# A head's 64 channels on 64 partitions from batch 3 on: VectorE and GpSimd exchange odd and even channels, one load for each head of a pair

## The chip, the cores and the metric

The kernel runs on one core of a Trainium2 chip. The metric is the time of one execution in microseconds on the device. The profile is of one execution, with times counted from the start of its span, which runs from the first to the last instruction. TensorE does the matrix products; its weight loads are listed beside its matmuls as an engine of their own (PEld). ScalarE (ACT) does exponentials, the activation and most copies out of PSUM, VectorE (DVE) transposes, masks and normalises, GpSimd (POOL) adds and converts, and SyncE (SP) issues transfers, as GpSimd does for its own queue.

## The reference

Inputs are `q`, `k` and `v` of shape 8 batches x 8 heads x 576 positions x 64 channels, and two weights, 512 x 2048 and 2048 x 512. For each batch and head two attentions are added, and the sum, with the heads side by side, goes through a two-layer network:

```
q_d, k_d, v_d = means over each 4 positions               # 144 positions
out_up    = repeat(softmax(scale * q_d k_d^T) v_d, 4)     # every position with every one
out_local = softmax(scale * q k^T, only |i - j| < 4) v    # a narrow band
x = (out_up + out_local), heads beside each other         # 4608 tokens x 512
out = gelu_quick(x @ w_in) @ w_out                        # h * sigmoid(1.702 h)
```

## The kernel before, in words

**Groups.** The network works on nine groups of 512 tokens. A group g is 16 steps of `mm1` (four matmuls each, `w_in` against `xT`, then an activation into `gT`), then 64 matmuls of `mm2` (`gT` against `w_out`, four rows of output, 16 matmuls each). All engines run in the order in which the program lists their instructions (a manual schedule); nothing is reordered by a planner. The attention of batch b = g + 1 is laid into group g: a dictionary `steps` holds functions by step number, 0 to 15 for the steps of `mm1` and 16 to 80 for the matmuls of `mm2`, and each function is listed ahead of its step. `POS` (L893) gives the steps of the six parts of an attention, `POS_G` exceptions by group: scores of the first four heads (`qd` 0) at 13, their exponentials and masks at 16, scores and exponentials of the other four heads at 35, then the two value products with their normalisation at 44 and 58, then a change of the activation table at 65. Work for the next batch that is listed outside `steps` stands ahead of the group's matmuls on its engine.

**Scores.** `load_1` (L187) brings four heads of q or k, 4 x 576 x 64 numbers, into a tile of 128 partitions x 1152: a head on 32 partitions, each with 18 positions of 64 channels, converted to bf16 on the way. `prep_1` (L265) has VectorE transpose 32 x 32 blocks of pairs of channels (as 32-bit words). Then tile `kT` or `qT` holds on partition 32 r + d, for each position, the channels 2d and 2d + 1 of head r. A score therefore needs two matmuls with 32 rows, even channels then odd channels, added in PSUM (`score`, L365). `scores_mixed` (L409) lists for four heads 5 chunks x 2 halves (`par`) of the band, 64 keys x 60 queries, and 3 chunks of the means, 64 keys x 144 queries (`score_d`, L382), each twice: 80 + 24 = 104 matmuls. They sit in eight tiles of the array, four of 32 rows by two of 64 columns.

**What feeds them.** `pool_qk` (L293) has GpSimd add four positions to one, for k into `kdT` and for q into `qdT`. `prep_v` (L307) converts v to bf16, `prep_v4` (L311) adds v by fours, both on GpSimd. In the body for a later batch b (L1018 to L1031) the order is: `prep_v(b)`, the transposes and sums of `qd` 0, the loads of batch b + 1 (`load_v` on SP's queue, four of `load_1` on GpSimd's), the transposes and sums of `qd` 1, `prep_v4(b)`. The loads `load_v4(b + 1)` (SP's queue, 12 transfers) are listed one step after the last part of the attention, at 66.

The buffers that matter: `kb`/`qb` (loaded) two each by `qd`; `kT`, `qT`, `qdT` one each by `qd`; `vf` and `v4` one each; converted `vbs` and `vds` two each, by the batch's parity. PSUM has three pairs of banks (`PA`) for the attention and two banks (`PM`) for the network.

Of the kernel before, what the change touches and what calls it, by code (L numbers as in the profile page):

```python
# [9 lines left out]
BF16 = mybir.dt.bfloat16  # L10
# [9 lines left out]
def kernel(  # L20
# [16 lines left out]
    n_ffc = d_ff // 128  # L37
    n_groups = B * S // TG
    inv_sqrt_d = 1.0 / math.sqrt(D)
    KSTART = (0, 56)  # L40
    QSTART = (0, 60)

# [144 lines left out]
    def load_1(name, src, store, b, qd):  # L187
        t = ldp.tile(
            [128, 1152], BF16, name=f"{name}b{qd}", tag=f"{name}b{qd}", bufs=2
        )  # L190
        nc.gpsimd.dma_start(
            out=t,
            in_=bass.AP(
                tensor=src.tensor, offset=src[b, 4 * qd].offset,
                ap=[[1152, 128], [1, 1152]],
            ),
        )
        store[b, qd] = t

    def load_qk(b, qd):  # L200
        load_1("k", k, kf, b, qd)
# [63 lines left out]
    def prep_1(name, b, qd):  # L265
# [6 lines left out]
        )  # L272
        dst[b, qd] = tt

    def prep_qk(b, qd):
        prep_1("k", b, qd)
        prep_1("q", b, qd)
# [30 lines left out]
        cp = eng.copy if eng is nc.scalar else eng.tensor_copy  # L308
        cp(out=vbs[b % 2][:, i, h, 0:D], in_=vf[b][:, i, h])  # L309

    def prep_v4(b, eng):  # L311
        for kc in range(3):
            x = v4[0:112, kc].rearrange("p h (f d) -> p h f d", f=4)
            t1 = work.tile([128, HP, 2, D], FP32, name="v2", tag="v2")
            eng.tensor_tensor(  # L315
                out=t1[0:112], in0=x[:, :, 0:2, :], in1=x[:, :, 2:4, :], op=ALU.add
            )
            eng.tensor_tensor(
                out=vds[b % 2][0:112, kc, :, 0:D],
                in0=t1[0:112, :, 0, :], in1=t1[0:112, :, 1, :], op=ALU.add,  # L320
            )
# [87 lines left out]
    def scores_mixed(b, qd, sp, sd):  # L409
        for i in range(5):  # L410
            for a in range(2):
                if i >= 2:
                    for r in range(4):
                        score_d(b, qd, sd, i - 2, a, r)
                for x in (1, 0):
                    for r in range(4):
                        score(b, qd, sp, i, a, (side(b, r)[0] + x) % 2, r)

    def exp_local(qd, sp):
        for u in range(2):  # L420
# [227 lines left out]
    def attention(b, slots=None):  # L648
        st = {}

        def s_pe(qd):
            if slots:
                st["s", qd], st["d", qd] = [ps_tile(), ps_tile()], ps_tile()
            else:
                st["s", qd], st["d", qd] = PA[1:3], PA[0]
            scores_mixed(b, qd, st["s", qd], st["d", qd])

        def s_act(qd):
            if qd == 0:
# [12 lines left out]

        def avn(*hps):
            def f():
                for hp in hps:
                    st["o", hp] = av(b, hp, slots and slots[hp % 2])
                for hp in hps:
                    st["y", hp] = normalise(st["o", hp])
            return f

        def tr():
            for u in range(2):
                st["x", u], st["x", u + 2] = x_pair(slots and slots[u])
# [206 lines left out]
        for f in steps.get(n, ()):  # L890
            f()

    POS = [13, 16, 35, 44, 58, 65]  # L893
    POS_G = {0: [16, 18, 29, 46, 58, 67], 5: [13, 16, 35, 48, 61, 66]}
    VDP_0 = 41

    o, y, x = {}, {}, {}
# [98 lines left out]
    for g in range(n_groups):  # L996
        b = g + 1
        if g == 0:
# [75 lines left out]
```

## Time and profile before

| What | Value |
|---|---|
| Three runs | 311.63, 314.28, 315.88 us; median 314.28 |
| Profiled execution | 311.98 us, of which span 310.2 us |
| Busy share of the span | PE 96%, ACT 67%, PEld 49%, POOL 44%, DVE 38% |
| One group with attention (122.20 to 154.44 us) | 32.24 us |
| TensorE clock granted | 0.999 of full |
| 32-row matmuls of scores (all batches) | 1280 of 32x60 and 384 of 32x144 |
| Queue of GpSimd's transfers | 18336 packets, 14.81 MB |

Rows of groups read: line, engine, operation, written tile `<-` read tiles, shape, count, busy time in us, mean ns of one, and then the idle time of the engine just ahead of them with what ended it. In a timeline the columns are start, length, engine, line, operation and count. A matmul's end is modelled and matmuls overlap, so starts are read, not ends.

### The profile page before, as it was taken

The numbers are of one execution on the slowest core, as the hardware profiler recorded it, in microseconds if no ns is written. First come the engines' busy times: TensorE is split into PE (matmuls) and PEld (weight loads), VectorE is DVE, ScalarE is ACT, GpSimd is POOL, SyncE is SP. The second block draws the span as 40 slices with busy tenths as digits, with TensorE's granted clock in tenths as the row PEclk, the third lists the DMA queues.
The fourth block names the chain that finished last, engine by engine and source line by source line (L and its number), as shares of the span: only waits on it lengthen the run. The fifth ranks groups of instructions, "written<-read, shape, count | busy, mean of one in ns | idle before, by whom it ended". The sixth has DMA issues, their size and how long they took to land.

```text
span 310.2 us, 9588 instructions
## 1 busy us (share of the span) xinstructions
PE 297.4 (96%) x4140; PEld 152.8 (49%) x4183; DVE 119.4 (38%) x273; ACT 209.1 (67%) x349; POOL 137.7 (44%) x168
## 2 busy tenths in 40 slices
PE   7789999999999999999999999999999999999995
PEld 3465445455544555445545554545454544444444
DVE  5983626801592149303850286026901630000000
ACT  5557771867886788768966896688858876316611
POOL 8764790479149920992089216932492000000000
PEclk9999999999999999999999999999999999999999
DMA  6999999899959933995299609991620110010011
GB/s 135 147 200 208 178 134 212 161 193 244 175 176 194 189 90 114 193 187 124 83 199 201 136 36 203 207 168 39 165 58 35 39 70 0 34 68 36 0 68 68
DMA packets 64650, 40.07 MB, mean 129 GB/s; under 512 B 44640, under 2 KB 56032, under 8 KB 64608
## 3 DMA queue, kind: packets, MB, share of 16 engines
q0 software_dynamic: 18336, 14.81, 34.4%
q1 hardware_dynamic: 45600, 24.46, 33.5%
q8 instruction: 32, 0.52, 0.8%
q10 hardware_dynamic: 672, 0.20, 0.3%
q14 instruction: 10, 0.08, 0.1%
HBM read 44.83 MB, written 9.44 MB: 175 GB/s over the span
## 4 chain that ended last, share of the span: by engine, by line
PE 91%; DVE 2%; DMA 2%; issue 2%; ACT 1%; POOL 0%; ACTq 0%; POOLq 0%
PE pm L864 36%; PE pm L800 36%; PE pa L800 4%; PE pa L745 4%; PE pa L369 3%; PE pa L385 2%; DMA qb<-in_q_dram 2%; PE pa L864 2%; PE pm L879 1%; DVE qT L269 1%; ACT od L614 1%; PE pm L644 0%; DVE kT L269 0%; DVE qdT L288 0%; DVE kdT L288 0%
## 5 line engine op out<-in xcount | busy, mean ns | idle before, releaser
L800 PE MATMUL pm<-xT,w_in_bf 128*128 128x512 bf16 x496 | 118.2, 379 | 1.6 <-ACT xT L607 0.5
L864 PE MATMUL pm<-w_out_bf,gT 128*128 128x512 bf16 x505 | 114.6, 379 | 3.3 <-issue 3.2
L811 ACT ACTIVATE gT<-pm 128x512 bf16<-128x512 f32 x128 | 76.3, 598 | 43.5 <-PE pm L800 43.5
L800 PEld LDWEIGHTS <-w_in_bf 128*128 128x128 bf16 x576 | 55.6, 98 | 67.0 <-issue 1.2
L864 PEld LDWEIGHTS <-gT 128*128 128x128 bf16 x560 | 52.8, 98 | 61.8 <-issue 0.5
L435 DVE TENSOR_TENSOR es<-es,mask 128x600 bf16<-128x600 bf16 x28 | 14.2, 510 | 95.6 <-ACT es L421 94.5
L849 ACT ACTIVATE osb<-pm 128x512 f32<-128x512 f32 (+2 forms) x35 | 20.2, 581 | 24.4 <-PE pm L864 19.0
L299 POOL TENSOR_TENSOR pq<-kT 128x576 f32<-128x576 bf16 x13 | 15.1, 1164 | 45.8 <-DVE kT L269 45.8
L763 DVE TENSOR_TENSOR xT<-pa,r 128x300 bf16<-128x300 f32 (+3 forms) x96 | 24.0, 303 | 19.5 <-ACT r L758 19.2
L309 POOL CAST vb<-vf 128x2560 bf16<-128x2560 f32 x6 | 13.9, 2320 | 31.8 <-DMA vf<-in_v_dram 19.9
L421 ACT ACTIVATE es<-pa 128x600 bf16<-128x600 f32 x32 | 19.7, 668 | 9.0 <-PE pa L369 8.9
L757 ACT ACTIVATE r<-pa 128x504 f32<-128x504 f32 (+1 forms) x36 | 20.6, 572 | 4.3 <-PE pa L745 4.3
L315 POOL TENSOR_TENSOR v<-v 112x512 f32<-112x512 f32 x18 | 23.0, 1280 | 0.0
L758 ACT ACTIVATE r<-r 128x504 f32<-128x504 f32 (+1 forms) x36 | 22.2, 616 | 1.1
L269 DVE STREAM_TRANSPOSE kT<-kb 128x576 f32<-128x576 f32 x16 | 19.9, 1245 | 6.3 <-DMA kb<-in_k_dram 6.2
L851 DVE TENSOR_SCALAR osb<-pm 128x128 f32<-128x128 f32 x1 | 0.3, 292 | 55.4 <-ACT osb L849 55.4
L269 DVE STREAM_TRANSPOSE qT<-qb 128x576 f32<-128x576 f32 x16 | 19.8, 1239 | 0.5 <-DMA qb<-in_q_dram 0.5
L800 PE MATMUL pa<-xT,w_in_bf 128*128 128x512 bf16 x63 | 19.6, 379 | 0.0
L369 PEld LDWEIGHTS <-kT 32*64 32x64 bf16 x1280 | 14.6, 104 | 8.0 <-issue 4.5
L369 PE MATMUL pa<-qT,kT 32*64 32x60 bf16 x1280 | 16.8, 198 | 1.7 <-DVE qT L269 1.5
L771 DVE TENSOR_TENSOR xT<-xT,ydt 128x576 bf16<-128x576 bf16 x24 | 17.9, 787 | 0.0
L222 POOL DMA_DIRECT2D vb<-in_v_dram x18 | 12.3, 697 | 8.8 <-DMA w_in_bf<-in_moe_w_in_dram 3.6
(105 smaller groups left out, 288.7 us busy)
## 6 DMA issues: line engine op xcount, KB each, us to landing
out_dram<-osb SPq DMA_DIRECT2D x35, 256.0 KB, 3.0
vf<-in_v_dram SPq DMA_DIRECT2D x61, 128.0 KB, 6.4
v<-in_v_dram SPq DMA_DIRECT2D x72, 96.0 KB, 3.2
kb<-in_k_dram POOLq DMA_DIRECT2D x16, 288.0 KB, 7.4
qb<-in_q_dram POOLq DMA_DIRECT2D x16, 288.0 KB, 9.0
w_in_bf<-in_moe_w_in_dram POOLq DMA_DIRECT2D x4, 512.0 KB, 7.7
w_out_bf<-in_moe_w_out_dram POOLq DMA_DIRECT2D x4, 512.0 KB, 12.3
vb<-in_v_dram POOLq DMA_DIRECT2D x18, 64.0 KB, 6.6
```

The source lines that it names most:

```text
L269: nc.vector.transpose(out=t32.rearrange("p (i c) -> p c i", c=18), in_=store[b, qd].bitcast(FP32).rearrange("p (c d) -> p c d", c=18),)
L315: eng.tensor_tensor(out=t1[0:112], in0=x[:, :, 0:2, :], in1=x[:, :, 2:4, :], op=ALU.add)
L369: nc.tensor.matmul(sp[r // 2][64 * par : 64 * par + 64, r % 2, 60 * i : 60 * i + 60], lhsT=kT[b, qd][rows, k0 : k0 + 64, a], rhs=qT[b, qd] ...
L421: nc.scalar.activation(out=es[2 * qd + u][:, :, 0:300], in_=sp[u][:, :, 0:300], func=AF.Exp, scale=inv_sqrt_d,)
L757: nc.scalar.activation(out=r, in_=den, func=AF.Ln)
L758: nc.scalar.activation(out=r, in_=r, func=AF.Exp, scale=-1.0)
L763: nc.vector.tensor_tensor(out=sub(x[u], t0 + at, (114, n), (1, c)), in0=sub(src, c0, (60, n), (1, c)), in1=sub(rc, c0, (60, n), (1, c)), o ...
L771: nc.vector.tensor_tensor(out=xx, in0=xx, in1=yd[:, u, :, None].to_broadcast([128, SD, 4]), op=ALU.add,)
L800: nc.tensor.matmul(acc, lhsT=w_in_bf[:, dmc, ffc * 128 : (ffc + 1) * 128], rhs=xT[dmc][:, g * TG : g * TG + TG], start=(dmc == 0), stop=(d ...
L811: nc.scalar.activation(out=gT[:, ffc, :], in_=acc, func=AF.Silu, scale=GELU_SCALE)
L849: eng.activation(out=osb, in_=ap, func=AF.Copy, scale=1.0 / GELU_SCALE)
L864: nc.tensor.matmul(ops[t], lhsT=gT[:, ffc, t * 128 : (t + 1) * 128], rhs=w_out_bf[:, ffc, :], start=(ffc == 0), stop=(ffc == n_ffc - 1),)
```

## The change

From batch 3 on (`WIDE = 3`) the four heads of a quarter tile stand otherwise. Each `kb` or `qb` tile is now loaded by two transfers, each of 64 partitions: transfer j brings heads j and j + 2 of the four. After the transpose the first 32 of these partitions hold head j, the next 32 head j + 2, with even and odd channels as before. `keep_odd` has GpSimd copy the odd channels of all 128 partitions aside. `swap` has VectorE copy the even channels of head j + 2 over the odd channels of head j, and then the kept odd channels of head j over the even channels of head j + 2, with partitions shifted by 32. Then place u = 0, 1 of a position holds all 64 channels of head 2u + j on 64 partitions. `scores_64` needs one matmul of 64 rows for each product: 40 for the band and 12 for the means, 52 instead of 104, in four tiles of 64 x 64.

The work is listed in another order: the transposes, `keep_odd` and `prep_v` of the next batch's first half stand at step 17 of the group before (after the masks of `qd` 0), and the loads for them first in that group; `swap` and the sums come at the start of the group; the loads of `qd` 1 stand at the end of GpSimd's work; `prep_v4` is split around the sums of `qd` 1; `load_v4` moves from step 66 to 48; scores of `qd` 1 move from step 35 to 34, and group 5 loses its own positions (48, 61, 66 become 44, 58, 65). For the odd copies and the shifted copies of ten halves (batches 3 to 7) 20 instructions come to GpSimd and 80 to VectorE, and GpSimd issues 20 transfers more.

```diff
+    WIDE = 3
@@ load_1
+        if b < WIDE:
+            nc.gpsimd.dma_start(out=t, in_=bass.AP(... ap=[[1152, 128], [1, 1152]]))
+            return
+        for j in range(2):
+            nc.gpsimd.dma_start(
+                out=t[64 * j : 64 * j + 64],
+                in_=bass.AP(
+                    tensor=src.tensor, offset=src[b, 4 * qd + j].offset,
+                    ap=[[2 * S * D, 2], [1152, 32], [1, 1152]],
+                ),
+            )
@@
+    def keep_odd(b, qd):
+        for name, src in (("k", kT), ("q", qT)):
+            t = work.tile([128, S], BF16, name="odd", tag="odd")
+            nc.gpsimd.tensor_copy(out=t, in_=src[b, qd][:, :, 1])
+            odd[name] = t
+
+    def swap(b, qd):
+        for name, src in (("k", kT), ("q", qT)):
+            tt = src[b, qd]
+            for p in (0, 64):
+                nc.vector.tensor_copy(out=tt[p : p + 32, :, 1], in_=tt[p + 32 : p + 64, :, 0])
+            for p in (0, 64):
+                nc.vector.tensor_copy(out=tt[p + 32 : p + 64, :, 0], in_=odd[name][p : p + 32])
@@
+    def scores_64(b, qd, sp, sd):
+        def local(u, j, par, i):
+            rows = slice(64 * j, 64 * j + 64)
+            k0, q0 = 114 * i + KSTART[par], 114 * i + QSTART[par]
+            nc.tensor.matmul(
+                sp[u][64 * par : 64 * par + 64, j, 60 * i : 60 * i + 60],
+                lhsT=kT[b, qd][rows, k0 : k0 + 64, u],
+                rhs=qT[b, qd][rows, q0 : q0 + 60, u],
+                start=True, stop=True, tile_position=(64 * j, 64 * par),
+            )
+
+        def down(u, j, kc):
+            rows = slice(64 * j, 64 * j + 64)
+            nc.tensor.matmul(
+                sd[64 * u : 64 * u + 64, j, SD * kc : SD * kc + SD],
+                lhsT=kdT[qd][rows, 48 * kc : 48 * kc + 64, u],
+                rhs=qdT[b, qd][rows, :, u],
+                start=True, stop=True, tile_position=(64 * j, 64 * u),
+            )
+
+        for u in range(2):
+            for i in range(5):
+                for x in range(2):
+                    for j in range(2):
+                        local(u, j, (j + x) % 2, i)
+        for kc in range(3):
+            for x in range(2):
+                for j in range(2):
+                    down((j + x) % 2, j, kc)
@@ attention
-            scores_mixed(b, qd, st["s", qd], st["d", qd])
+            (scores_mixed if b < WIDE else scores_64)(b, qd, st["s", qd], st["d", qd])
@@
-    POS = [13, 16, 35, 44, 58, 65]
-    POS_G = {0: [16, 18, 29, 46, 58, 67], 5: [13, 16, 35, 48, 61, 66]}
+    POS = [13, 16, 34, 44, 58, 65]
+    POS_G = {0: [16, 18, 29, 46, 58, 67], 1: [13, 16, 35, 44, 58, 65]}
@@ body of a group
-        elif b < B:
-            if g > 1:
-                prep_v(b, nc.gpsimd)
+        elif b < WIDE:
             prep_qk(b, 0)
             pool_qk(b, 0)
-            if g == 1:
-                prep_v(b, nc.gpsimd)
-            if b + 1 < B:
-                load_v(b + 1)
-                for qd in range(NQ):
-                    load_qk(b + 1, qd)
+            load_qk(b + 1, 0)
+            prep_v(b, nc.gpsimd)
+            load_v(b + 1)
             prep_qk(b, 1)
             pool_qk(b, 1)
             prep_v4(b, nc.gpsimd)
+            load_qk(b + 1, 1)
+        elif b < B:
+            if b + 1 < B:
+                load_qk(b + 1, 0)
+                load_v(b + 1)
+            swap(b, 0)
+            pool_qk(b, 0)
+            prep_qk(b, 1)
+            keep_odd(b, 1)
+            swap(b, 1)
+            prep_v4(b, nc.gpsimd, (0,))
+            pool_qk(b, 1)
+            prep_v4(b, nc.gpsimd, (1, 2))
+            if b + 1 < B:
+                load_qk(b + 1, 1)
@@ steps
-                steps.setdefault(pos[-1] + 1, []).append(lambda: load_v4(b + 1))
+                for n, f in (
+                    (17, lambda: prep_qk(b + 1, 0)),
+                    (17, lambda: keep_odd(b + 1, 0)),
+                    (17, lambda: prep_v(b + 1, nc.gpsimd)),
+                    (48, lambda: load_v4(b + 1)),
+                ):
+                    steps.setdefault(n, []).append(f)
```

More of the change, by code (lines that the diff above doesn't have):

```diff
@@ L190, in load_1 @@
         )
[L191 to L197, printed above, removed]
-        store[b, qd] = t
+        store[b, qd] = t
+        if b < WIDE:
+            nc.gpsimd.dma_start(
+                out=t,
+                in_=bass.AP(
+                    tensor=src.tensor, offset=src[b, 4 * qd].offset,
+                    ap=[[1152, 128], [1, 1152]],
+                ),
+            )
+            return
+        for j in range(2):
+            nc.gpsimd.dma_start(
+                out=t[64 * j : 64 * j + 64],
+                in_=bass.AP(
+                    tensor=src.tensor, offset=src[b, 4 * qd + j].offset,
+                    ap=[[2 * S * D, 2], [1152, 32], [1, 1152]],
+                ),
+            )
     def load_qk(b, qd):
@@ L273, in prep_1 @@
         dst[b, qd] = tt
+    odd = {}
+    def keep_odd(b, qd):
[10 more added lines that the diff above has]
+                nc.vector.tensor_copy(out=tt[p + 32 : p + 64, :, 0], in_=odd[name][p : p + 32])
     def prep_qk(b, qd):
@@ L309, in prep_v, with prep_v4 @@
         cp(out=vbs[b % 2][:, i, h, 0:D], in_=vf[b][:, i, h])
-    def prep_v4(b, eng):
-        for kc in range(3):
+    def prep_v4(b, eng, kcs=range(3)):
+        for kc in kcs:
             x = v4[0:112, kc].rearrange("p h (f d) -> p h f d", f=4)
@@ L417, in scores_mixed @@
                         score(b, qd, sp, i, a, (side(b, r)[0] + x) % 2, r)
+    def scores_64(b, qd, sp, sd):
[15 more added lines that the diff above has]
+                start=True, stop=True, tile_position=(64 * j, 64 * u),
+            )
+        for u in range(2):
[7 more added lines that the diff above has]
+                    down((j + x) % 2, j, kc)
     def exp_local(qd, sp):
```

## The prediction

> **What bounds the kernel.** First the page's busy shares and the chain that ended last.
>
> ```profile
> span 310.2 us, 9588 instructions
> PE 297.4 (96%) x4140; PEld 152.8 (49%) x4183; DVE 119.4 (38%) x273; ACT 209.1 (67%) x349; POOL 137.7 (44%) x168
> ...
> PE 91%; DVE 2%; DMA 2%; issue 2%; ACT 1%; POOL 0%; ACTq 0%; POOLq 0%
> ```
>
> TensorE is on the chain for 91% of the span; VectorE and GpSimd are nowhere on it between 60 and 306 us. So time is won where TensorE's own work shrinks, and lost where one of the others makes it wait. Two slices of the busy time by stretch, both from group 3 (122.20 to 154.44 us, batch 4), show a score stage:
>
> ```profile
> 133.35:134.33 0.98, 0.98 (x105) 0.94 (x104) 0.00 (x0) 0.60 (x1) 0.98 (x1) 1.00 1.11 205
> 141.13:142.15 1.02, 1.02 (x105) 0.98 (x105) 0.00 (x0) 0.42 (x1) 0.00 (x0) 1.00 0.63 138
> ```
>
> Columns are stretch, length, then busy time and count of PE, PEld, DVE, ACT, POOL, clock, DMA share, GB/s. Each stretch goes from the first weight load of the scores to the first weight load of the dense matmuls behind. I took the same stretch, by the weight loads of the timeline, for the ten score stages of batches 3 to 7: 0.98, 1.11, 0.98, 1.02, 1.04, 0.98, 0.99, 0.99, 0.98, 0.99, together 10.06 us. That is all that the change can shrink.
>
> **The score stage, before.** In the timeline twelve matmuls with their weight loads (8 of the band, 4 of the means) repeat every 0.100 to 0.105 us, as in
>
> ```profile
> 101.40 0.23 PE L385 MATMUL pa<-qdT,kdT 32*64 32x144 bf16 x2
> ...
> 101.50 0.24 PE L385 MATMUL pa<-qdT,kdT 32*64 32x144 bf16 x2
> ...
> 101.60 0.24 PE L385 MATMUL pa<-qdT,kdT 32*64 32x144 bf16 x2
> ```
>
> that is 8.4 ns for a matmul, however many columns it has; the 32 band matmuls ahead of them start at 101.04 and the next part at 101.31, 8.4 ns each too. So the pace is one of instructions, 4.2 ns each, and 104 x 8.4 = 0.87 us; the other 0.11 us of 0.98 is the end of the stage.
>
> **The score stage, after.** 52 matmuls in four tiles of 64 x 64. The trace has that form in the value product of batch 1:
>
> ```profile
> 46.63 0.34 PE L443 MATMUL pa<-vb,es 64*64 64x65 bf16 x17
> ...
> 46.99 0.33 PE L443 MATMUL pa<-vb,es 64*64 64x65 bf16 x17
> ```
>
> These are the first matmuls of two lots of forty: 0.36 us, 9 ns each, 36 ns for each tile's turn. The columns alone take less: a dense matmul of 512 columns comes every 0.216 us (29 in 6.26 us on the chain), 2.37 columns a ns, so 65 take 27 ns. The 40 band matmuls (60 columns) cost 40 x 9 = 0.36 us. The 12 of the means put three of 144 columns on each tile; 3 x 144 / 2.37 = 0.18 us, and in the later value products (L745) twelve such start between 144.73 and 144.95, 0.22. I take 0.20. With the same 0.11 at the end: 0.67 us. Ten stages: 10.06 - 6.7 = **3.4 us less**. Ends: columns alone, (600 + 432) / 2.37 = 0.435 + 0.11 = 0.55, gives 4.6 us; the whole L745 stage's pace, 76 matmuls in 1.09 us (144.20 to 145.29), 14.3 ns each, gives 0.75 and 2.6 us. The value taken is the one from the row with the same columns.
>
> One rule of the Trainium skill speaks against this step (TensorE: Matmul & The Clock Gate, Part 3): weight loads overlap running matmuls only in another row group, and the change halves the row groups. By it the stage would lengthen only where neighbours share rows; the listed order alternates the two row halves, as that of L443 does, whose 9 ns show the overlap, so the trace bears the sum out here.
>
> **What is added beside TensorE.** Rows:
>
> ```profile
> L435 DVE TENSOR_TENSOR es<-es,mask 128x600 bf16<-128x600 bf16 x28 | 14.2, 510 | 95.6 <-ACT es L421 94.5
> L480 DVE TENSOR_TENSOR y<-pa,rc 128x896 bf16<-128x896 f32 x4 | 4.4, 1090 | 0.1
> L763 DVE TENSOR_TENSOR xT<-pa,r 128x3 bf16<-128x3 f32 x24 | 3.7, 152 | 0.0
> L309 POOL CAST vb<-vf 128x2560 bf16<-128x2560 f32 x6 | 13.9, 2320 | 31.8 <-DMA vf<-in_v_dram 19.9 <-DMA out_dram<-osb 10.4 <-DMA v<-in_v_dram 1.6
> L299 POOL TENSOR_TENSOR pq<-qT 128x576 f32<-128x576 bf16 x14 | 16.0, 1145 | 0.1
> ```
>
> VectorE's shifted copy of 32 x 576 is not in the trace. L480 and L763 give (1090 - 152) / 893 = 1.05 ns for an element and 149 ns: 0.75 us; L435 at 510 ns for 600 is the fast end, some 0.50. Back-to-back operations start 0.13 to 0.16 us sooner than their lengths say (transposes of 1.24 us start 1.08 apart). I take 0.65 from start to start, near the slow end, since the elements are not dense. GpSimd's odd copy: 0.6 by L309 (0.9 ns an element), 1.15 by L299; I take 0.8.
>
> The group of batch 4, in us after its start, where transposes now stand from 122.31 to 126.81 and then VectorE is idle for 12.95 us:
> - VectorE: normalisation of the batch before ends at +0.2 (the last L771). Swap of `qd` 0, eight copies, to +5.4; transposes of `qd` 1 to +7.6.
> - GpSimd: sums (1.15 + 0.67) of k +2.8 to +4.7, of q +5.4 to +7.2. Score stage 0 needs them at +11.2: 4 us to spare. Odd copies of `qd` 1 to +8.8.
> - VectorE: swap of `qd` 1 from +8.0 to +13.2. Masks come behind it only at +17.5 (139.75), so nothing queues.
> - GpSimd: first third of `prep_v4` (1.27 + 0.73) to +10.8, sums of k to +12.7, of q +13.2 to **+15.1**. Score stage 1 stood at +18.9 (141.13); one step of 0.22 and 0.33 of the first stage earlier, +18.4: **3.3 us to spare**.
> - GpSimd then: two thirds of `prep_v4` to +19.1, four issues of 0.57 to +21.4 (two tiles in two transfers each), odd copies of the next batch to +23 (their transposes, behind the masks, end at +20.8), `prep_v` 2.3 to +25.3, four issues to +27.6. The group lasts 31.6.
>
> So 16 x 0.65 on VectorE (13.8 busy in 32.24 now) and 4 x 0.8 plus 4 x 0.57 on GpSimd (17.5 now) cost nothing while they lie in idle time. The transposes at step 17 stand ahead of the second masks (143.19) and of the normalisation (146.07); they would have to be over 2 us late to move these. The issue waits of SP: `vf` is now free a third of a group earlier (its conversion ends at +25.3), `load_v4` waits for `prep_v4` at +19.1 and is listed at about +22, so the stores behind it do not wait. Positions 34 for 35, and group 5's, only move matmuls past each other: nothing, with 0.3 us either way.
>
> **Sum.** 311.98 (profiled execution) - 3.4 = 308.6. The profiled execution lies 2.3 below the median of the runs (314.28), whose spread is 4.25; on the median's footing the time is **310.9**.
>
> **Rivals.**
> 1. *The stage doesn't shrink.* If the four tiles run one behind another more than L443 shows, 52 matmuls cost up to 19 ns each and nothing is won: 313.5 to 314.3. For it: half as many tiles; against it: L443.
> 2. *It shrinks more.* Behind the second score stage the first dense matmul starts 0.23 us after its weight load (142.15, 142.38), which may be TensorE's queue of 208 instructions; with the columns-only stage, 0.55, that makes 4.6 + 5 x 0.23 = 5.8 less: 308.5.
> 3. *The second swap is late* (the case that ends slower). VectorE and GpSimd disturb each other:
>
> ```profile
> 75.16 1.54 DVE L435 TENSOR_TENSOR es<-es,mask 128x600 bf16<-128x600 bf16 x2 [13.37 <-ACT es L421]
> 75.54 0.84 POOL L318 TENSOR_TENSOR vd<-v 112x256 bf16<-112x256 f32 x1
> ...
> 76.33 1.49 POOL L315 TENSOR_TENSOR v<-v 112x512 f32<-112x512 f32 x1
> ```
>
> Two masks take 1.03 us undisturbed, 1.54 here; GpSimd's take 0.72 and 1.27 undisturbed. With copies 1.5 times (0.97) and GpSimd 1.2 times as long wherever both work: q of `qd` 0 swapped at +6.7, odd copies to +10.8, `qd` 1 swapped from +9.9 to +17.7, its sums at +19.9, 1.5 us late in each of five groups: 7.5 - 3.4 = +4.1, **318.4**. It decides from a copy of some 0.85 us on. Against it: that everything is disturbed at once.
> 4. *A load is late.* Two transfers of 144 KB where one of 288 KB was. Now a load lands in 4.7 to 12.8 us (median 7.4 for kb), four of them taking 21.1% of 16 engines for 33 us, 14 engine-us for a half. If a half ran on two engines only, that is 7 us alone, 14 beside as much other traffic; `qd` 1 has from +21.4 to the next group's +5.4, 15.6 us, and 3.3 to spare behind. Beyond 19 us it costs: 22 us would give 5 x 3 - 3.4, 325.9. The Trainium skill (DMA: Bandwidth & Descriptors, Rules for kernel authors, and How many engines) advises one transfer over 128 partitions against two halves, and takes the number of engines to divide both patterns' slowest dimension, here 2 of the source; no run here shows that yet.
>
> **Chances.** Forecast 0.72; (1) 0.09; (2) 0.05; (3) 0.09; (4) 0.05. What a measurement here can tell from no change is about 2%, 6.3 us: 308.0 and 320.6. The forecast's own ends, 309.7 to 311.7, widen by the runs' spread, about 2 either way, and by a footing between the profiled execution and the median. The range reaches from 306.8 (rival 2 on the faster footing) to 316.0 (half of rival 3): it leaves out most of (3) and (4). Faster by over 2%: 0.08 (half of (2), and the forecast on a faster footing). Slower: 0.08 (the worse half of (3) and most of (4)). Within: 0.84.
>
> **What will show it.** Score stages of batches 3 to 7 as one line group of 64 x 64, 400 of 60 columns and 120 of 144, weight load to dense weight load 0.67 us; groups of 31.6 instead of 32.2 to 32.5. Sums of q for `qd` 1 over 2 us ahead of the second stage. No wait of TensorE for kT, qT or qdT. A copy line over 0.85 us, a kb landing over 16 us, or such a wait on the chain would make the prediction wrong.

## The result

The changed kernel takes 316.71 us (median of 18 runs, 315.18 to 317.9) against 313.62 us (18 runs, 311.63 to 315.88): 1.0096 times as long, interval 1.0071 to 1.0121. Forecast were 310.9 us and a gain; the time lies above the range. Both profiled executions are some 1.6 us below their medians (before 311.98, after 315.19), so the two traces may be set against each other. The page of the changed kernel, its counts and the chain that ended last:

```profile
span 313.4 us, 8712 instructions
...
PE 301.9 (96%) x3663; PEld 149.3 (48%) x3663; DVE 197.7 (63%) x353; ACT 208.6 (67%) x349; POOL 173.0 (55%) x208
...
PE 64%; DVE 16%; POOL 8%; issue 4%; DMA 3%; ACT 3%; POOLq 0%; DVEq 0%; ACTq 0%
```

TensorE held 91% of the chain before and holds 64% now; VectorE and GpSimd, which had 2%, have 24%. VectorE's busy time rose from 119.4 to 197.7 us. Its 80 copies take 60 of these 78; the rest is old work that became longer.

Where the 3 us went, by the first dense matmul of each group (us):

| | group 2 starts | group 2 | 3 | 4 | 5 | 6 | behind |
|---|---|---|---|---|---|---|---|
| before | 89.91 | 32.34 | 32.24 | 32.51 | 32.39 | 32.18 | 58.6 |
| after | 90.05 | **36.13** | 31.99 | 32.10 | 32.10 | 32.41 | 58.6 |
| forecast | | 31.6 | 31.6 | 31.6 | 31.6 | 31.6 | |

Against the forecast's 31.6 group 2 loses 4.5 us and the four others 0.4, 0.5, 0.5 and 0.8: 6.7 us, which is the gap from -3.4 to +3.2. So two losses are to be explained.

**The score stage itself** did as forecast. Two stretches from the first weight load of the scores to the next dense one (columns as in the prediction), and the matmuls of the first:

```profile
137.34:137.99 0.65, 0.65 (x54) 0.54 (x53) 0.62 (x2) 0.55 (x1) 0.65 (x1) 1.00 1.05 247
144.57:145.28 0.71, 0.71 (x54) 0.60 (x53) 0.71 (x1) 0.71 (x3) 0.71 (x1) 1.00 0.00 0
```

```profile
137.34 0.52 PE L450 MATMUL pa<-qT,kT 64*64 64x60 bf16 x40
137.68 0.37 PE L459 MATMUL pa<-qdT,kdT 64*64 64x144 bf16 x12
137.99 0.39 PE L857 MATMUL pm<-xT,w_in_bf 128*128 128x512 bf16 x1
```

0.34 us for the forty of the band, 0.31 to the next dense one, 0.65 where 0.98 had been.

**Group 2.** GpSimd's timeline there (start, length, engine, line, operation; in brackets its idle time ahead and what ended it):

```profile
93.16 2.32 POOL L336 CAST vb<-vf 128x2560 bf16<-128x2560 f32 x1 [11.18 <-DMA out_dram<-osb]
95.43 1.31 POOL L203 DMA_DIRECT2D kb<-in_k_dram  x2
96.71 1.53 POOL L203 DMA_DIRECT2D qb<-in_q_dram  x2
98.23 1.18 POOL L326 TENSOR_TENSOR pq<-kT 128x576 f32<-128x576 bf16 x1
...
101.95 0.66 POOL L291 COPY odd<-kT 128x576 bf16<-128x576 bf16 x1
...
109.68 1.43 POOL L326 TENSOR_TENSOR pq<-qT 128x576 f32<-128x576 bf16 x1 [0.94 <-DVE qT L300]
111.19 0.77 POOL L330 TENSOR_TENSOR qdT<-pq 128x288 bf16<-128x288 f32 x1
```

Listed in group 1, the conversion of v of batch 3 starts only 3.1 us into group 2, after 11.18 us of waiting (the brackets name an output transfer; the chain has a transfer from 88.36 to 93.18 just ahead, and the last load of v was issued at 88.3). Behind it stand four issues, the first sums at 98.23, forecast at 92.9, the odd copies of `qd` 1, the exchange that needs them (VectorE 102.64 to 109.60) and the last sum, done at 111.96. The means of the second score stage start at 112.01. The pause also cost clock, the share of TensorE's full speed that it was granted. The same columns as above, in stretches of 1 us:

```profile
111.00:112.00 1.00, 0.00 (x0) 0.00 (x0) 1.00 (x2) 0.28 (x1) 0.92 (x3) 0.70 1.06 205
112.00:113.00 1.00, 0.99 (x14) 0.51 (x14) 1.00 (x2) 0.36 (x1) 1.00 (x1) 0.50 0.74 128
113.00:114.00 1.00, 1.00 (x4) 0.38 (x3) 1.00 (x2) 0.53 (x1) 0.92 (x3) 0.50 0.21 42
```

TensorE had no dense matmul from 109.0 to 112.5 and nothing at all for 1.83 us ahead of 112.01. The granted clock falls in that pause, is 0.50 for over 2 us behind it, and the ten dense matmuls from 112.59 on take 3.38 us instead of 2.16.

**The other groups.** Rows of groups after, whose answers before were 510 ns (masks), 787 (sums of 576 columns), 1145 (`pq` of q) and 2320 (conversion):

```profile
L492 DVE TENSOR_TENSOR es<-es,mask 128x600 bf16<-128x600 bf16 x28 | 25.2, 934 | 24.5 <-ACT es L478 24.3
...
L828 DVE TENSOR_TENSOR xT<-xT,ydt 128x576 bf16<-128x576 bf16 x24 | 25.1, 1085 | 0.0
...
L326 POOL TENSOR_TENSOR pq<-qT 128x576 f32<-128x576 bf16 x14 | 16.3, 1165 | 8.5 <-DVE qT L300 8.4
L336 POOL CAST vb<-vf 128x2560 bf16<-128x2560 f32 x6 | 14.2, 2368 | 11.2 <-DMA out_dram<-osb 11.2
...
L298 DVE COPY qT<-qT 32x576 bf16<-32x576 bf16 x20 | 16.9, 847 | 0.6
```

VectorE's masks and sums, which read and write SBUF alone, became up to 1.8 times as long in the mean, GpSimd's operations far less (most the sums of k, 1164 to 1331). The timeline shows what they meet (group 3; lines of both engines):

```profile
152.32 3.56 DVE L828 TENSOR_TENSOR xT<-xT,ydt 128x576 bf16<-128x576 bf16 x2
...
152.22 2.38 POOL L336 CAST vb<-vf 128x2560 bf16<-128x2560 f32 x1
```

Two sums, 1.42 us where GpSimd is idle, take 3.56. The first alone takes 2.90, from 152.32 to 155.22: it begins 0.1 us behind the conversion and ends 0.6 us after it (154.60), and the second takes its usual 0.74. The chain has 2.03 us there in which nothing is shown to be waited for. Behind them come the other value product's normalisation and the sums which end the batch, and with these `xT` of the next group. Group 6 holds no conversion; it inherits a late start from group 5 (its exchange begins 1.5 us into the group), and its value product waits for the sums of v.

### The profile page after: what moved, and what is told of

It reads as the page before. It is cut to its first block, busy times and chain, and to the rows that moved or that the text cites. A ratio compares the mean times of both kernels' runs of the same rounds, so it can differ in the third digit from the quotient of the medians.

```text
span 313.4 us, 8712 instructions
## 1 busy us (share of the span) xinstructions
PE 301.9 (96%) x3663; PEld 149.3 (48%) x3663; DVE 197.7 (63%) x353; ACT 208.6 (67%) x349; POOL 173.0 (55%) x208
## 4 chain that ended last, share of the span: by engine, by line
PE 64%; DVE 16%; POOL 8%; issue 4%; DMA 3%; ACT 3%; POOLq 0%; DVEq 0%; ACTq 0%
PE pm L921 26%; PE pm L857 23%; PE pa L857 4%; DVE kT L298 3%; DVE qT L298 3%; PE pa L802 3%; POOL pq L326 3%; DVE qT L300 2%; DMA qb<-in_q_dram 2%; DVE kT L300 2%; POOL v L342 2%; PE pa L921 2%; DVE xT L828 2%; DVE xT L820 2%; DMA out_dram<-osb 2%
## 5 line engine op out<-in xcount | busy, mean ns | idle before, releaser
L921 PE MATMUL pm<-w_out_bf,gT 128*128 128x512 bf16 x528 | 120.4, 382 | 0.0
L492 DVE TENSOR_TENSOR es<-es,mask 128x600 bf16<-128x600 bf16 x28 | 25.2, 934 | 24.5 <-ACT es L478 24.3
L326 POOL TENSOR_TENSOR pq<-kT 128x576 f32<-128x576 bf16 x13 | 17.3, 1331 | 33.3 <-DVE kT L300 24.2
L342 POOL TENSOR_TENSOR v<-v 112x512 f32<-112x512 f32 x18 | 25.3, 1404 | 0.2 <-DMA vf<-in_v_dram 0.2
L828 DVE TENSOR_TENSOR xT<-xT,ydt 128x576 bf16<-128x576 bf16 x24 | 25.1, 1085 | 0.0
L478 ACT ACTIVATE es<-pa 128x600 bf16<-128x600 f32 x32 | 19.9, 679 | 5.8 <-PE pa L396 5.3
L326 POOL TENSOR_TENSOR pq<-qT 128x576 f32<-128x576 bf16 x14 | 16.3, 1165 | 8.5 <-DVE qT L300 8.4
L280 DVE STREAM_TRANSPOSE qT<-qb 128x576 f32<-128x576 f32 x16 | 19.9, 1241 | 0.6 <-DMA qb<-in_q_dram 0.4
L298 DVE COPY kT<-kT 32x576 bf16<-32x576 bf16 x20 | 15.5, 773 | 4.2 <-POOL odd L291 3.7
L298 DVE COPY qT<-qT 32x576 bf16<-32x576 bf16 x20 | 16.9, 847 | 0.6
## 6 DMA issues: line engine op xcount, KB each, us to landing
kb<-in_k_dram POOLq DMA_DIRECT2D x20, 144.0 KB, 11.1
qb<-in_q_dram POOLq DMA_DIRECT2D x20, 144.0 KB, 12.8
```

The lines of the kernel that those rows point to most:

```text
L280: nc.vector.transpose(out=t32.rearrange("p (i c) -> p c i", c=18), in_=store[b, qd].bitcast(FP32).rearrange("p (c d) -> p c d", c=18),)
L298: nc.vector.tensor_copy(out=tt[p : p + 32, :, 1], in_=tt[p + 32 : p + 64, :, 0])
L326: nc.gpsimd.tensor_tensor(out=t1, in0=sv[:, :, 0:2, :], in1=sv[:, :, 2:4, :], op=ALU.add)
L342: eng.tensor_tensor(out=t1[0:112], in0=x[:, :, 0:2, :], in1=x[:, :, 2:4, :], op=ALU.add)
L492: nc.vector.tensor_tensor(out=ev, in0=ev, in1=mask, op=ALU.mult)
L828: nc.vector.tensor_tensor(out=xx, in0=xx, in1=yd[:, u, :, None].to_broadcast([128, SD, 4]), op=ALU.add,)
```

## The experiments

The numbers in brackets behind a ratio are its interval; all ratios are to the kernel before. The first dense matmul of group 2 stood at 89.9 to 92.8 us in the profiled executions, whatever the kernel, so I compare lengths of groups rather than totals where I can.

**Wide scores alone.** The upper bound: what does TensorE's part win if nothing is added? In the kernel before:

```diff
-            scores_mixed(b, qd, st["s", qd], st["d", qd])
+            (scores_mixed if b < WIDE else scores_64)(b, qd, st["s", qd], st["d", qd])
```

(`WIDE` and `scores_64` are added as in the change and not shown again.)

> The kernel before with nothing changed but the score matmuls: from batch 3 on 52 of 64 rows. Nothing is exchanged, so each product of batches 3 to 7 takes channels of two heads and is another one; loads, sums, order and positions are those of before. If the step of the prediction holds (10.06 us of score stages become 6.7): 3.4 us less, ratio 0.989. If the smaller stages are eaten by what follows (ScalarE's exponentials, the next wait): under 1.5 us, ratio 0.995 or more.

310.88 us, ratio 0.9873 [0.9826, 0.992]; groups 31.58, 31.58, 31.57, 31.77, 31.58. TensorE's part is worth what the prediction said (31.6). Its page:

```profile
span 307.7 us, 8591 instructions
...
PE 92%; DVE 2%; DMA 2%; ACT 1%; issue 1%; POOL 0%; DVEq 0%; ACTq 0%; POOLq 0%
```

**The exchange left out**, all else as changed:

```diff
-            swap(b, 0)
@@
-            keep_odd(b, 1)
-            swap(b, 1)
@@ step 17
-                    (17, lambda: keep_odd(b + 1, 0)),
```

> The changed kernel without the exchange: VectorE's copies between quarters and GpSimd's copies of the odd elements are left out, so that the scores from batch 3 on mix channels of two heads; the loads in halves, the order of the lists and the wide scores stay. Theory A (the copies, and what they do to VectorE and GpSimd, are the loss): groups 3 to 5 take 31.6 us as in the kernel before with wide scores alone, and group 2's stall shrinks to under 1.5 us, since 1.4 us of odd copies and 7 us of exchange no longer stand behind the late conversion; total 309 to 312. Theory B (the halves and the late v are the loss): group 2 still takes 34 to 36 us, total 314 to 316.

312.05 us, ratio 0.9935 [0.9906, 0.9964]; groups 31.58, 31.58, 31.57, 33.48, 31.58. Group 2's stall needs the exchange behind the late conversion. But group 5 still loses 1.9 us: just ahead of its start a pair of sums of 576 columns took 3.54 us beside the conversion and the next pair 2.80 beside GpSimd's own sums, and TensorE waits 1.6 us for them. So GpSimd's work holds VectorE without any exchange; whether the conversion hits a sum depends on when it starts, here after waits of 1.6 to 11.6 us.

**The conversion of batch 3 moved behind**, into group 2, after the odd copies of `qd` 1; later batches as changed. The lines that move `load_v` and the first third of `prep_v4` of batch 3 with it are left out here:

```diff
+            if b > WIDE:
+                prep_v4(b, nc.gpsimd, (0,))
+            else:
+                prep_v(b, nc.gpsimd)
+                load_v(b + 1)
             pool_qk(b, 1)
@@ ... @@ step 17
-                    (17, lambda: prep_v(b + 1, nc.gpsimd)),
+                    (17, lambda: prep_v(b + 1, nc.gpsimd) if b >= WIDE else None),
```

> The changed kernel, but the conversion of v of batch 3 stands in group 2 behind the odd copies of qd 1 (in the place of the first third of prep_v4) instead of at step 17 of group 1; the loads stay in halves. Theories A and C: GpSimd no longer sits ahead of the sums, group 2 falls to 32 to 33 us, the time by 3 to 4 us, ratio 0.998 to 1.001. Theory B: no change beyond 0.5 us, ratio 1.010.

315.46 us, ratio 1.0046 [1.0016, 1.0076]. Group 2 takes 34.12 instead of 36.13: the first sums start 2.3 us into the group, and the scores no longer wait. The stall turned into another, in the value product, which waits up to 2.1 us for the sums of v, now behind the conversion on GpSimd. The other groups take 32.45 to 32.77.

**Whole loads**: one transfer of 128 partitions for a tile. The two heads that then share 64 partitions are neighbours, so the heads of a pair are named anew, and the means go to two tiles of the array instead of four, listed between the matmuls of the band.

```diff
-        for j in range(2):
-            nc.gpsimd.dma_start(out=t[64 * j : 64 * j + 64], ...)
+        nc.gpsimd.dma_start(out=t, in_=bass.AP(..., ap=[[1152, 128], [1, 1152]]))
@@ scores_64
-                sp[u][64 * par : 64 * par + 64, j, 60 * i : 60 * i + 60],
+                sp[j][64 * par : 64 * par + 64, u, 60 * i : 60 * i + 60],
```

> The changed kernel with the loads of the kernel before: one contiguous transfer of 128 partitions for each tile; the heads of a pair are then 2j and 2j + 1 instead of j and j + 2, so that the 12 matmuls of the means stand in two of the four tiles, between those of the band. Theory A (the loss is one stall of group 2, because the halves' small packets hold up v of batch 3, on whose conversion GpSimd sits with the sums behind it): group 2 falls from 36.1 to about 32 us, v of batch 3 has landed by about 88 instead of 93.2, the time falls by 3 to 4 us, to a ratio of about 0.998 to before. Theory B (the loss is VectorE and GpSimd slowing each other in every group): group 2 and the time stay, ratio 1.010. Theory C (v of batch 3 is late because its transfers are listed later on SP's queue, whatever the packets): the conversion still starts at about 93, ratio 1.010.

319.44 us, ratio 1.011 [1.0026, 1.0193]. Group 2 takes 32.11, its stall is gone: v of batch 3 is converted at 86.49 instead of 93.16. But groups 3 to 5 take 34.21, 33.70 and 33.69. In the middle of group 4 the second pair of masks takes 5.16 us, while GpSimd goes through two odd copies and the conversion; the value product waits for the normalisation behind it. The 0.53 us between 32.11 and 31.58 is the score stages', with two tiles for the means: 0.83 and 1.06 us where 0.65 and 0.71 had been.

**The same, with the conversion listed behind the issue of the next loads:**

```diff
@@ group's start, b >= WIDE
+            prep_v(b, nc.gpsimd)
             if b + 1 < B:
@@ step 17
-                    (17, lambda: prep_v(b + 1, nc.gpsimd)),
```

> As the first of these kernels (whole loads), and the conversion of v stands behind the issue of the next loads instead of ahead of it, some 2.7 us later, where VectorE works out of PSUM. If VectorE's sum of 576 columns (two operands in SBUF) waits for GpSimd's conversion to end, the 3.5 us pair becomes 1.5 us, the 0.2 to 0.4 us waits at the start of each group go, and the time is 1 to 1.5 us under the first kernel's. If not, the two are alike within 0.5 us.

319.2 us, ratio 1.0142 [1.0091, 1.0194], so the expected gain did not come. Groups: 32.11, 32.12, **37.30**, 32.11, 32.11. All of the loss is in one group, where a mask took 5.8 us while GpSimd went through four issues, two odd copies and the conversion without a gap; in the group behind it the odd copies waited 0.5 and 0.4 us for the transposes, and the pair of masks took 1.30. Moving the conversion only moves what it hits.

**The conversion in five instructions**, at the same place:

```diff
-                    (17, lambda: prep_v(b + 1, nc.gpsimd)),
+                    (17, lambda: [prep_v(b + 1, nc.gpsimd, i) for i in range(5)]),
```

> The changed kernel, with GpSimd's conversion of v written as five instructions, one for each chunk of 64 positions, instead of one of 2.4 us. Everything else stands as it was. Theory A (a VectorE instruction that reads SBUF twice waits for the GpSimd instruction that runs, and no longer): the pair of 576-column sums that meets the conversion falls from 3.55 to at most 2.4 us (1.42 and one or two pieces of 0.5), and groups 3 to 5 lose up to 0.3 us each where they are bound by it. Theory B (VectorE stands back until GpSimd's queue has a gap): the pair stays at 3.3 to 4.0 us, since five pieces back to back leave none, and the groups keep 32.0 to 32.4. Under both group 2 keeps its stall (35.5 to 36.5 us), since v of batch 3 lands no earlier; total 316.7 +- 1.

312.66 us, ratio 0.9961 [0.9916, 1.0007]. Groups 34.43, **31.58, 31.67, 31.71, 31.57**. Its timeline in group 4:

```profile
183.73 2.00 DVE L828 TENSOR_TENSOR xT<-xT,ydt 128x576 bf16<-128x576 bf16 x2
...
183.36 3.96 POOL L336 CAST vb<-vf 128x512 bf16<-128x512 f32 x5
```

The pair of sums falls from 3.56 to 2.00 us, and GpSimd's five pieces take 3.96 where those of a run below take 3.08: here the engines take turns. Theory A holds for this pair and those of groups 3 and 5, and the one long instruction was the whole loss of groups 3 to 6, all four of which go to the value of the wide scores alone, within 0.1 us. The Trainium skill (SBUF — State Buffer, "SBUF: two separate sides") has VectorE and GpSimd share a pair of ports under an exclusive lock which whoever starts first holds for a whole instruction. The trace agrees here: a sum of 0.75 us took 2.90 beside the one conversion, and the two take 0.92 and 1.16 beside its pieces, longer by less than a piece of 0.62. It does not agree everywhere: in group 2 of this run a sum took 2.58 us, passed over by two odd copies and two pieces.

Group 2 is no better in substance: its pieces wait for `vf` by name, 6.61 us the longest, the last still stands at 95.07 and the sums behind it begin at 98.20, as before the split; the group is shorter by 1.7 us since in this execution it began 1.6 us later, at 91.63.

**Whole loads with the conversion in five**, to see whether the masks follow the same rule:

> The kernel of the run with whole loads (one transfer of 128 partitions for a tile, heads of a pair named anew), with GpSimd's conversion of v as five instructions instead of one and nothing else changed. There the second of a pair of masks took 4.8 us in group 3's second half, while GpSimd ran two odd copies of 0.68 and the conversion of 2.33 without a gap. Theory A (VectorE waits for the one GpSimd instruction that runs): the longest mask falls to at most 1.5 us, groups 3 to 5 from 33.7 to 34.2 to 32.1 us, total near 313. Theory B (VectorE can stand back over several GpSimd instructions in a row, the masks more than the sums): a mask of 3 us or more appears again and groups 3 to 5 stay above 33 us, total 317 to 321.

318.82 us, ratio 1.0181 [1.0065, 1.0298]; groups 32.10, 34.54, 34.04, 34.04, 32.11. Theory B holds. Group 4's timeline, both engines:

```profile
180.02 5.50 DVE L481 TENSOR_TENSOR es<-es,mask 128x600 bf16<-128x600 bf16 x2
...
180.91 0.68 POOL L281 COPY odd<-kT 128x576 bf16<-128x576 bf16 x1
181.51 0.68 POOL L281 COPY odd<-qT 128x576 bf16<-128x576 bf16 x1
182.12 3.08 POOL L326 CAST vb<-vf 128x512 bf16<-128x512 f32 x5
```

The longest mask takes 4.71 us: it begins at 180.0 and ends at about the end of the fourth piece, having stood back over two issues, two odd copies and four pieces of 0.61 to 0.68 us, none of which was slowed. So VectorE does not always get its turn when one instruction ends, as it mostly did above, and a lock of one instruction, as the Trainium skill has it, is too short for these masks. In the three traces with such a mask (this one, and both runs with whole loads before it) it began while GpSimd was issuing a transfer. That is not the whole condition: other masks that began so took their 0.46 us, and the sum of 2.58 us above began in an odd copy. What decides it I did not test.

**v by ScalarE**, in five pieces of 0.6 us between the activations of the group's own `mm1`:

```diff
@@ body of a group
-                load_v(b + 1)
@@ step 17
-                    (17, lambda: prep_v(b + 1, nc.gpsimd)),
@@
+            if g and b >= WIDE:
+                for i in range(5):
+                    steps.setdefault(4 + 2 * i, []).append(lambda i=i: prep_v(b, nc.scalar, i))
+                if b + 1 < B:
+                    steps.setdefault(13, []).append(lambda: load_v(b + 1))
```

> The changed kernel with v of batches 3 to 7 converted by ScalarE, in five pieces between the silus of the same group's first matmul part, and not by GpSimd one group ahead; the load of the next v is issued behind the fifth piece. Loads in halves and exchange stay. Theory A (the conversion on GpSimd is behind both losses: in group 2 it waits for v ahead of the sums, in the others it holds VectorE): group 2 falls from 36.1 to 32 to 32.8 us, groups 3 to 5 from 32.1 to 31.6 to 31.9, total 310 to 313. Theory B (the rest of GpSimd's work holds VectorE as much, or the halves are late): groups stay over 32, group 2 over 34. A third way: five pieces of about 0.6 us don't fit into ScalarE's 0.27 us between two silus; then the first part of each group gets up to 1.5 us longer, and TensorE waits for silu.

310.04 us, ratio 0.9895 [0.9832, 0.9958], groups 31.82 or 31.83, all five. Both losses are gone, and the sums take 747 to 754 ns, none longer. The third way costs 0.24 us a group.

**The same with whole loads:**

> The same with whole loads of 128 partitions, as in the run with whole loads, in place of halves. Theory A: the stalls of that run in groups 3 to 5 (33.7 to 34.2 us), where the pair of masks stood 4 to 5 us behind odd copies and conversion, go with the conversion: masks at most 2.5 us, groups 31.6 to 32.0, total 309.5 to 312, below the kernel before. Theory B (VectorE stands back for any GpSimd work): masks still take over 4 us in some groups, total 315 to 319.

314.05 us, ratio 1.002 [0.9987, 1.0052], groups all 32.36. No stall is left, as theory A has it, but the expected total was wrong: it forgot that the score stages of the whole loads had cost 0.53 us a group, as measured above. 31.58 + 0.24 + 0.53 = 32.35.

**Halves of consecutive rows.** Two transfers of 64 partitions as in the change, but each with two neighbouring heads, so that the source has one level of rows (heads named anew as above):

```diff
-                    tensor=src.tensor, offset=src[b, 4 * qd + j].offset,
-                    ap=[[2 * S * D, 2], [1152, 32], [1, 1152]],
+                    tensor=src.tensor, offset=src[b, 4 * qd + 2 * j].offset,
+                    ap=[[1152, 64], [1, 1152]],
```

> The changed kernel, but with each half of a load taking 64 consecutive rows of 1152 values (two whole heads) in place of two rows of heads that are two apart; the heads of a pair are named anew, as in the run with whole loads, with its score stage. One conversion of v on GpSimd as in the changed kernel. Theory A (a half load is cut into 288-byte packets because its source has two levels of rows): packets of the software queue fall from 36.6 thousand to near 18.3 thousand, landing from 11 to 13 us to 6 to 9 us, v of batch 3 is converted 3 us or more earlier and group 2's stall is under 1.5 us. Theory B (64 partitions instead of 128 make it so): packets and landing stay, and group 2 takes 35 to 37 us.

312.89 us, ratio 0.9976 [0.9941, 1.001]; groups 32.12, 32.12, 32.12, 32.12, 32.11. The queue of GpSimd's transfers and the landing of its halves (KB each, median us), first the changed kernel's page, then this one's:

```profile
q0 software_dynamic: 36576, 14.89, 37.0%
...
kb<-in_k_dram POOLq DMA_DIRECT2D x20, 144.0 KB, 11.1
```

```profile
q0 software_dynamic: 18656, 14.82, 35.5%
...
kb<-in_k_dram POOLq DMA_DIRECT2D x20, 144.0 KB, 3.7
```

Theory A holds: it is the two levels of rows, not the halves; landing fell further than expected. What the packets are, the traces list one by one. In all three kernels 4096 packets of this queue carry a row of 2304 bytes. All of the difference is packets of 4 bytes: 928 before, 1248 with plain halves, 19168 in the changed kernel, whose 18240 packets more carry only 0.08 MB. A whole tile goes as 128 rows and 16 such packets, a plain half as 64 and 16, a half with two levels as 64 and 464.

The starts of the rows show the rest. Wherever the four halves of a `qd` stand alone in the changed kernel (256 rows, four times), the rows fall into eight strings, in each of which one row starts as the one ahead ends; four plain halves, or two whole tiles, make 15 to 17 strings. So a half with two levels seems to run on two engines where the other forms spread over all sixteen. The count fits: 528 is 16 x 33, which is 32 rows and a closing packet on two engines, and as many packets of 4 bytes on each of the other fourteen. No view names the engine of a packet, so this stays worked out from starts and counts.

And v, which goes through another queue, is held up. SP's ten issues for v of batch 3, in the changed kernel's timeline and in this one's:

```profile
72.15 16.11 SPq L222 DMA_DIRECT2D vf<-in_v_dram  x10
```

```profile
71.72 7.58 SPq L214 DMA_DIRECT2D vf<-in_v_dram  x10
```

The conversion starts at 86.39 instead of 93.16. Whether the two engines or the short packets slow SP's issues, no run separates. (The kernel before needed 15.09 us for these issues as well, but began at 68.44, 3.7 us earlier in its order, and converted at 87.38.) The score stage of whole loads is in the 32.12; no group loses more. The conversion, though one instruction, all but misses the sums here: from group 2 on it stands directly behind the odd copies, as in the changed kernel, but in group 3 it begins 24.8 us into the group and not 26.2, since GpSimd is done sooner (an issue takes some 0.54 us, not 0.67). It ends 0.3 us after the pair of sums begins, which takes 1.58 us.

**The old order**: the kernel before with halves, exchange and wide scores, nothing moved:

```diff
             prep_qk(b, 0)
+            if b >= WIDE:
+                keep_odd(b, 0)
+                swap(b, 0)
             pool_qk(b, 0)
@@
             prep_qk(b, 1)
+            if b >= WIDE:
+                keep_odd(b, 1)
+                swap(b, 1)
             pool_qk(b, 1)
```

> The kernel before with loads in halves, exchange and wide scores from batch 3 on, in its own order of the lists: transposes, odd copies, exchange and sums all stand at a group's start, v converted ahead of them, nothing moved into the group before; only the change's positions and moves are undone. Theory A (the moves are needed: the first score stage stands 11.5 us behind the group's start, the second 17 us, and VectorE and GpSimd need some 10 to 12 us for a half of the heads): both score stages of groups 2 to 5 wait, 1 to 4 us in sum, groups 33 to 36 us, total 318 to 328. Theory B (idle time covers it as the prediction has it): groups of 31.6 to 32.2, total 310 to 313.

350.14 us, ratio 1.1128 [1.1048, 1.1209]; groups 41.2, 39.9, 39.9, 39.1, 36.9, worse than either theory. From the chain and, below it, from the list of waits (us in all, times, longest):

```profile
PE 40%; POOL 20%; DVE 19%; issue 7%; ACT 5%; DMA 4%; SPq 3%; POOLq 0%; DVEq 0%
```

```profile
POOL odd L291 <- DVE kT L280: 37.5, 5, 8.8
...
DVE kT L298 <- POOL odd L291: 22.2, 5, 5.5
...
PE pa L450 <- DVE qT L300: 11.7, 8, 3.3
```

Odd copies need transposes, the exchange needs odd copies, the sums the exchange: on two engines in order these wait in turn. The granted clock fell to 0.961 in the mean, which is in the loss as well. The moves in the change are what makes the exchange bearable: with them the same work takes 316.71 us.

**Both cures**: v of batch 3 by ScalarE as above, that of later batches on GpSimd in five instructions, halves and exchange as changed. (The line that keeps `load_v` of the next batch from being listed twice in group 2 is left out here.)

```diff
-                    (17, lambda: prep_v(b + 1, nc.gpsimd)),
+                    (17, lambda: g > 1 and [prep_v(b + 1, nc.gpsimd, i) for i in range(5)]),
@@
+            if b == WIDE:
+                for i in range(5):
+                    steps.setdefault(4 + 2 * i, []).append(lambda i=i: prep_v(b, nc.scalar, i))
+                steps.setdefault(13, []).append(lambda: load_v(b + 1))
```

> The changed kernel with the two cures of the runs before put together: v of batch 3 alone is converted by ScalarE, in five pieces in group 2's first matmul part, with the load of the next v behind the fifth; v of batches 4 to 7 stays on GpSimd one group ahead, in five instructions instead of one. Theory A (two separate losses: the late v in front of the sums in group 2, the 2.4 us conversion in front of VectorE's sums in the others): group 2 takes 31.8 to 32.0 us as with ScalarE, groups 3 to 6 31.6 to 31.7 as with the split; from group 2's start to the end 216.9 to 217.5 us, total 308.5 to 310.5, ratio 0.983 to 0.990. Theory B (the split helped group 3 and on only because group 2's stall had moved the transfers): a group of 33 us or more appears again, total over 311.

309.7 us (308.74 to 310.9), ratio **0.9865** [0.9816, 0.9913], faster than both kernels. Groups 31.83, 31.57, 31.58, 31.59, 31.57.

```profile
span 308.6 us, 8746 instructions
...
PE 298.9 (97%) x3663; PEld 148.5 (48%) x3663; DVE 187.4 (61%) x353; ACT 210.5 (68%) x354; POOL 176.4 (57%) x223
...
PE 91%; DMA 4%; ACT 1%; issue 1%; POOL 1%; DVE 0%; POOLq 0%; DVEq 0%; ACTq 0%
```

From group 2's start to the end it takes 308.6 - 91.83 = 216.8 us, before 310.2 - 89.91 = 220.3: 3.5 us less. The exchange's 80 copies and the 4-byte packets are all still there, and hidden.

## Why the prediction was wrong

- **The stage, 0.67 us, and ten stages, 3.4 us: right.** Measured 0.65 and 0.71; the wide scores alone give groups of 31.58 to 31.77 for 31.6, and with both cures 3.5 us are won. Neither of the first two rivals occurred. The 0.23 us of the second was most likely a dense matmul missing from the record: the trace of before has 4140 matmuls for 4183 weight loads, that of after 3663 for 3663.
- **"Cost nothing while they lie in idle time": the step that failed, for groups 3 to 6.** The undisturbed sizes were fair: a copy 0.50 from start to start, odd copies 0.66 to 0.73 for 0.8. But I let only the copies suffer from GpSimd, and that as a rival, and costed every move of GpSimd's work by GpSimd's own clock. Moving `prep_v` to step 17 put an instruction of 2.38 us beside sums of VectorE that end a batch; it made a pair of these 2.1 us longer. A split of that instruction alone took the loss away.
- **"3.3 us to spare": too much.** In group 4 the exchange of `qd` 1 ended at +16.0 and the last sum at +18.0, forecast +13.2 and +15.1; the stage came at +18.5. Half a microsecond was left, not 3.3. The copies took 0.63 to 0.85 us in the mean by line, single ones up to 1.4 beside GpSimd's sums and 2.5 behind the late conversion. That is the third rival's mechanism; its point of decision was nearly reached, but not in group 4.
- **One group for all: the step that failed in group 2.** I followed the group of batch 4 and wrote "`prep_v` 2.3 to +25.3". For batch 3 that instruction waits for v; it ended 5.4 us into the next group, and first sums, odd copies, exchange and last sums, which I had begun at +2.8, began at +8.2. The page of before had the warning: its row of the conversion says 19.9 us of waiting for `vf`. The change put that wait ahead of a longer chain and did not make v come earlier.
- **Fourth rival, loads in halves: its condition seems to have held, but the victim was another.** The prediction asked what would follow if a half ran on two engines only, and the rows run as if it did. The landing it worked out from that, 7 us alone and 14 beside as much other traffic, fits: 9.3 to 15.5 us. So q and k landed in time (11.1 and 12.8 us in the median, under the 16 I had named), and SP's issues for v on another queue slowed instead, which no rival had. The rule for the number of engines that the prediction took from the Trainium skill (DMA: Bandwidth & Descriptors, How many engines) gives two here, and the trace agrees, by the eight strings of four halves. I had also leaned on the Trainium skill (DMA: Bandwidth & Descriptors, "Rules for kernel authors") against two halves as such: the runs show no price for them, 3.7 and 5.8 us for plain ones against 4.4 and 6.1 for whole tiles of the same batches.
- **The stores "do not wait", the step from 35 to 34:** no sign of either in the groups' lengths.

## What to carry to other kernels

Idle time on VectorE or GpSimd is no cover by itself: look at which instruction of the other engine runs at that moment, and split long GpSimd instructions that stand beside short VectorE work on a chain. Follow a moved step through the first batch as well as through a middle one, since there its input arrives latest, and every instruction behind it on an in-order engine inherits the wait. Look at the outermost level of a load's source: with a 2 there a half load of this case landed three times as late as with 64 rows in one level, and the queue that paid was another one.

## What the runs showed of the hardware

- VectorE stood back over two issues and six GpSimd instructions in a row (4.71 us, one mask of 0.46), and over four (2.58 us, one sum of 0.75), but took turns with five in another place (2.00 us for two sums of 0.75). What decides is open.
- Which operations suffer: masks, sums of two SBUF operands and the copies; transposes (1.25 us before, in and after such stretches) and operations that read PSUM did not change.
- A half load of 144 KB with two levels of rows, the outer of 2: 64 packets of 2304 bytes and 464 of 4 bytes, by their starts on two engines, and 11.1 us to landing; with one level 64 and 16 packets and 3.7 us.
- In a pause of TensorE of 1.83 us, with no dense matmul for 3.5 us, the granted clock fell, and it was 0.50 for over 2 us behind it.
- Forty matmuls of 64 x 64 tiles with 60 columns start within 0.34 us, 8.5 ns each, the pace of the 32-row ones before: spread over the tiles as here, their count sets the time and not their rows. With the 12 of the means on two of the four tiles, the same 52 take 0.83 and 1.06 us for 0.65 and 0.71.
